# Attention and an MLP on one core: from head pairs and a polynomial GELU to token blocks and a table GELU

## The chip, the cores and the metric

The kernel runs on one core of one Trainium2 chip. The metric is the device time of one execution in microseconds, lower is better. Time before: median 383.45 us of three runs (379.78, 383.45, 383.53).

The engines of the core are named as in the profile: PE is TensorE (matmuls and transposes), DVE is VectorE, ACT is ScalarE, POOL is GpSimd, SP is SyncE, which here only issues transfers. Each engine works through its own instructions in order and waits for others through semaphores.

## What is computed

A causal linear attention with a decay per head over blocks of tokens, followed by a two-layer MLP with a tanh GELU. Four sequences of 768 tokens, 8 heads of 64 dimensions, so 3072 tokens of 512 values; the hidden layer has 2048.

```python
def _attn_ref(q, k, v, lam):
    ...
    for b in range(nb):
        intra = np.einsum('bhic,bhjc->bhij', qb, kb) * Dmask[None]
        intra = np.einsum('bhij,bhjd->bhid', intra, vb)
        inter = np.einsum('bhid,bhde->bhie', qb * lam_pow[None], kv_state)
        out[:, :, sl] = intra + inter
        kb_dec = kb * rev_pow[None]
        kv_state = lam_block[None, :, None, None] * kv_state + np.einsum('bhsd,bhse->bhde', kb_dec, vb)

def _moe_ref(x, w_in, w_out):
    h = x @ w_in
    g = 0.5 * h * (1.0 + np.tanh(c * (h + 0.044715 * h * h * h)))
    return g @ w_out
```

The reference uses blocks of 64 tokens; both kernels use blocks of 128, which gives the same result. All inputs are float32; both kernels multiply in float16 and accumulate in float32.

## The kernel before

The unit of attention is a cell: one sequence, one block of 128 tokens, one pair of heads; there are 4 x 6 x 4 = 96. For each sequence and head pair, `prep_scale` (L177) scales q and k by powers of the decay on ScalarE and casts v on GpSimd; `prep_transpose` (L190) makes 12 transposes on TensorE and copies them out of PSUM on ScalarE. `cell_stage_a` (L207) multiplies q and k of a block (two matmuls, tile Sps) and applies the causal mask on VectorE (tile PT). `cell_stage_b` (L220) makes PT times v and the carried state times q, alternating in one PSUM tile OKV for the two heads, then the new state product; VectorE updates the state and copies the result into xT, the transposed MLP input for all 3072 tokens.

The MLP runs in jobs of 512 tokens (the last two of 256). `mm1` (L262) makes four accumulating matmuls into Hps for one of 16 hidden tiles. The GELU is spread over two engines: ScalarE copies Hps to h16 (L276), VectorE squares it and forms the cubic (L278, L281), ScalarE applies a sigmoid (L290), VectorE multiplies (L292). `mm2` (L295) makes 16 accumulating matmuls for 128 tokens, ScalarE copies them out (L306), SP issues the store.

Order: `pump` (L347) takes queued MLP entries up to a budget after each cell; `jobs_after` says after which block a job is queued. A job's second layer is deferred behind the first tiles of the next job. The framework's scheduler then orders each engine's instructions by its own cost model, keeping dependences. PSUM has two buffers each for Sps and Tps together, OKV and the MLP.

Loads: SP issues q, k and v of the first sequence head pair by head pair, in pieces of 192 KB (L82), later sequences in pieces of 384 KB. The weights come through GpSimd's queue: both halves of w_in (2 MB each, L96) at the very start, w_out in four parts of 1 MB later (L102), each into a buffer that gT also uses. ScalarE casts all weights.

## Time and profile before

| | |
|---|---|
| median of three runs | 383.45 us (379.78 to 383.53) |
| span of the profiled execution, first to last instruction | 380.5 us |
| TensorE busy, instructions | 313.5 us, 1760 |
| VectorE busy, instructions | 215.1 us, 642 |
| ScalarE busy, instructions | 208.0 us, 380 |
| GpSimd busy, instructions | 21.9 us, 47 |
| moved by DMA | 33.89 MB, mean 89 GB/s |
| mean granted TensorE clock | 0.937 |

The page gives the profiled execution's span and no separate time for it. In a row of the groups, the number after the bar is busy time in us, then the mean of one instruction in ns; after the second bar stands the idle time of the engine just before these instructions and what ended it. A timeline row gives start, duration, engine, line, operation and count. A busy TensorE is not one at its peak: matmuls overlap in its pipeline, so the distance between starts gives the pace. In the table of stretches the numbers after the stretch are its length, TensorE's busy time, its instructions, the granted clock, the DMA share and GB/s.

### The profile page before, as it was taken

Reading aid. Unit: us, or ns where it says so; the run is one execution under the profiler, and the core shown is the slowest. Engines: PE = TensorE matmul, PEld = TensorE weight load, DVE = VectorE, ACT = ScalarE, POOL = GpSimd, SP = SyncE. Lnnn points to the kernel's source line nnn. Section 1 sums busy time; section 2 is a strip of 40 time slices with the busy share of each in tenths; the row PEclk is TensorE's granted clock in tenths of the full one; section 3 lists DMA queues with packets and bytes.
Section 4 is the critical chain, followed back from the end, with each engine's and each line's share of the span. In section 5 each row is a group of like instructions: output and inputs, shape, how many; then the busy total and the mean of one; then the engine's idle time right before and its main releaser. Section 6 shows DMA issues by size and latency. Waiting matters only on the chain.

```text
span 380.5 us, 5045 instructions
## 1 busy us (share of the span) xinstructions
PE 313.5 (82%) x1760; PEld 153.2 (40%) x1760; DVE 215.1 (57%) x642; ACT 208.0 (55%) x380; POOL 21.9 (6%) x47
## 2 busy tenths in 40 slices
PE   0048099897899998999997799987999987995975
PEld 0024044443344444454444244543344444453542
DVE  3005034357998089743499551489641899118683
ACT  3793666638885166778366141676331566126663
POOL 2021202312000000310000000000000000000000
PEclk9999999999999999659999579999689997899989
DMA  7999999994800990001100002000001000020101
GB/s 276 312 224 286 274 279 218 213 218 76 167 1 13 228 202 2 0 3 56 55 2 1 0 2 83 29 1 0 2 28 57 28 1 3 28 83 2 54 2 57
DMA packets 79946, 33.89 MB, mean 89 GB/s; under 512 B 75312, under 2 KB 75312, under 8 KB 79408
## 3 DMA queue, kind: packets, MB, share of 16 engines
q1 hardware_dynamic: 78288, 25.18, 31.7%
q0 software_dynamic: 1632, 8.39, 6.0%
q8 instruction: 14, 0.23, 0.3%
q14 instruction: 12, 0.10, 0.1%
HBM read 27.27 MB, written 6.29 MB: 88 GB/s over the span
## 4 chain that ended last, share of the span: by engine, by line
PE 60%; DVE 17%; ACT 8%; SPq 7%; DMA 4%; issue 2%; ACTq 0%; DVEq 0%
PE O2ps L299 18%; PE Hps L268 15%; DVE u L281 7%; SPq L82 7%; PE OKV L227 6%; PE OKV L230 6%; DVE s L278 4%; PE Tps L198 4%; PE O2ps_t L299 4%; ACT h L276 4%; PE OKV L234 3%; ACT z L290 3%; PE Sps L213 3%; DVE gT L292 2%; DMA q<-in_q_dram 2%
## 5 line engine op out<-in xcount | busy, mean ns | idle before, releaser
L268 PE MATMUL Hps<-xT,w_in 128*128 128x512 f16 (+1 forms) x332 | 94.4, 413 | 12.8 <-ACT h L276 8.8
L290 ACT ACTIVATE z<-u 128x512 f16<-128x512 f16 (+1 forms) x112 | 63.2, 568 | 46.5 <-DVE u L281 45.3
L216 DVE TENSOR_TENSOR PT<-Sps,mask_all 128x256 f16<-128x256 f32 x96 | 39.9, 417 | 62.4 <-PE Sps L213 62.2
L299 PE MATMUL O2ps<-w_out,gT 128*128 128x512 f16 x304 | 70.2, 389 | 0.0
L281 DVE SCALAR_TENSOR_TENSOR u<-s,h 128x512 f16<-128x512 f16 (+1 forms) x112 | 67.5, 613 | 1.4
L276 ACT ACTIVATE h<-Hps 128x512 f16<-128x512 f32 (+1 forms) x83 | 48.2, 585 | 26.2 <-PE Hps L268 21.8
L268 PEld LDWEIGHTS <-w_in 128*128 128x128 f16 x448 | 41.5, 101 | 49.5 <-issue 18.6
L299 PEld LDWEIGHTS <-gT 128*128 128x128 f16 x384 | 38.0, 101 | 48.5 <-issue 5.8
L278 DVE TENSOR_TENSOR s<-h 128x512 f16<-128x512 f16 (+1 forms) x112 | 43.4, 387 | 24.8 <-ACT h L276 23.2
L198 PE MATMUL Tps<-ident,a 128*128 128x128 f16 x192 | 25.0, 279 | 35.0 <-ACT a L183 29.0
L227 PE MATMUL OKV<-PT,a 128*64 128x128 f16 x192 | 47.0, 266 | 5.7 <-DVE PT L216 5.3
L292 DVE TENSOR_TENSOR gT<-z,h 128x512 f16<-128x512 f16 (+1 forms) x112 | 42.7, 382 | 14.5 <-ACT z L290 14.2
L230 PE MATMUL OKV<-qkT,kv_new 64*64 64x128 f16 x160 | 42.8, 267 | 0.3
L306 ACT ACTIVATE o<-O2ps 128x512 f32<-128x512 f32 x19 | 11.3, 596 | 50.9 <-PE O2ps L299 49.0
L243 DVE CAST xT<-OKV 128x128 f16<-128x128 f32 x96 | 27.2, 283 | 19.0 <-PE OKV L234 19.0
L200 ACT ACTIVATE qkT<-Tps 128x512 f16<-128x512 f16 x48 | 27.3, 594 | 19.1 <-PE Tps L198 18.9
L227 PEld LDWEIGHTS <-a 128*64 128x64 f16 x192 | 20.5, 115 | 34.2 <-issue 22.6
L198 PEld LDWEIGHTS <-a 128*128 128x128 f16 x192 | 16.8, 124 | 42.3 <-ACT a L183 29.4
L238 DVE SCALAR_TENSOR_TENSOR kv_new<-kv_new,lam128vec,OKV 128x64 f16<-128x64 f16 x64 | 17.7, 276 | 27.1 <-PE OKV L234 26.9
L213 PE MATMUL Sps<-qkT 64*128 64x128 f16 x192 | 24.4, 250 | 2.1 <-ACT qkT L200 2.1
L230 PEld LDWEIGHTS <-kv_new 64*64 64x64 f16 x160 | 17.8, 111 | 19.2 <-issue 5.7
L183 ACT ACTIVATE a<-q,qdscale 128x384 f16<-128x384 f32 x32 | 19.1, 606 | 9.5 <-DMA q<-in_q_dram 9.1
(37 smaller groups left out, 163.2 us busy)
## 6 DMA issues: line engine op xcount, KB each, us to landing
out_dram<-o SPq DMA_DIRECT2D x24, 256.0 KB, 2.0
q<-in_q_dram SPq DMA_DIRECT2D x12, 384.0 KB, 6.1
k<-in_k_dram SPq DMA_DIRECT2D x12, 384.0 KB, 6.3
v<-in_v_dram SPq DMA_DIRECT2D x12, 384.0 KB, 6.1
wi<-in_moe_w_in_dram POOLq DMA_DIRECT2D x2, 2048.0 KB, 11.1
wo<-in_moe_w_out_dram POOLq DMA_DIRECT2D x4, 1024.0 KB, 7.2
q<-in_q_dram SPq DMA_DIRECT2D x8, 192.0 KB, 4.5
k<-in_k_dram SPq DMA_DIRECT2D x8, 192.0 KB, 4.5
```

The source lines that it names most:

```text
L198: nc.tensor.transpose(Tps[:, bip, t, :], a16[:, t, blk, :, :], ident[:])
L213: nc.tensor.matmul(Sps[:, hl, 0:P], qkT[hpart, blk, 1, :], qkT[hpart, blk, 0, :], start=True, stop=True)
L216: nc.vector.tensor_tensor(PT[:], Sps[:, :, 0:P], mask_all[:, h0 : h0 + 2, :], ALU.mult)
L227: nc.tensor.matmul(OKV[opart, 0:P], a16[:, 2, blk, hl, :], PT[:, hl, :], start=True, stop=(blk == 0))
L230: nc.tensor.matmul(OKV[opart, 0:P], kv16[(b, hp)][opart, :], qkT[opart, blk, 0, :], start=False, stop=True)
L268: nc.tensor.matmul(Hps[:, 0:ntok], w_in16[:, c, f * P : (f + 1) * P], xT[:, c, tok0 : tok0 + ntok], start=(c == 0), stop=(c == 3))
L276: nc.scalar.activation(out=h16[:, 0:ntok], in_=Hps[:, 0:ntok], func=AF.Copy)
L278: nc.vector.tensor_tensor(s16[:, 0:ntok], h16[:, 0:ntok], h16[:, 0:ntok], ALU.mult)
L281: nc.vector.scalar_tensor_tensor(u16[:, 0:ntok], s16[:, 0:ntok], C_ADD, h16[:, 0:ntok], ALU.add, ALU.mult)
L290: nc.scalar.activation(out=z16[:, 0:ntok], in_=u16[:, 0:ntok], func=AF.Sigmoid, scale=C_SIG)
L292: nc.vector.tensor_tensor(job["gT"][:, f, 0:ntok], z16[:, 0:ntok], h16[:, 0:ntok], ALU.mult)
L299: nc.tensor.matmul(O2[:], gT[:, f, tau * P : (tau + 1) * P], w_out16[:, f, :], start=(f == 0), stop=(f == NF - 1))
```

## The change

The kernel is rewritten around steps. A step is one block of 128 tokens of one sequence over all 8 heads; there are 24. Each step has three stages: `stage_t` makes eight transposes (q and k of four head pairs) into one PSUM tile and VectorE copies it out in one instruction; `stage_s` makes eight matmuls and VectorE masks all 1024 columns in one instruction; `stage_o` makes the eight PT products, the eight state products, then the eight state-times-q products, after which VectorE updates the state (four instructions) and ScalarE copies the result to xT. Step s has stage_t of block s + 2, stage_s of s + 1 and stage_o of s. Each of these PSUM tiles has one buffer, the MLP has three.

The MLP runs per group of 512 tokens in pieces of four matmuls: 16 first-layer pieces, each with its GELU, and 16 second-layer pieces. `fill` places eight pieces in each step from the sixth on (five in the fifth), in three portions ahead of the stages. What is left runs at the end. The GELU is one ScalarE activation from PSUM to gT; h16, s16, u16 and z16 are gone. VectorE copies the second layer out, GpSimd issues the stores.

`prep` works per pair of blocks: VectorE scales q, GpSimd scales k, ScalarE casts v, one instruction per block over all heads.

```diff
-    def load_split(b, hp):
-        for hl in range(2):
-            for t_x, x in ((t_q, q), (t_k, k), (t_v, v)):
-                nc.sync.dma_start(out=t_x[:, hl], in_=x[b, h0 + hl].rearrange(
-                    "(blk p) d -> p blk d", p=P))
...
+    def load_pair(b, bp):
...
+        for j in range(2):
+            r0 = (2 * bp + j) * P
+            for t, src in zip(ts, (q, k, v)):
+                nc.sync.dma_start(out=t[:, j], in_=src[b, :, r0 : r0 + P, :].rearrange(
+                    "h p d -> p h d"))
...
+        for blk in range(2):
+            nc.vector.tensor_tensor(
+                tq[:, blk], q32[:, blk],
+                qd[:].unsqueeze(2).to_broadcast([P, H, D]), ALU.mult)
+            nc.gpsimd.tensor_tensor(
+                tk[:, blk], k32[:, blk],
+                kd[:].unsqueeze(2).to_broadcast([P, H, D]), ALU.mult)
+            nc.scalar.activation(out=tv[:, blk], in_=v32[:, blk], func=AF.Copy)
...
-            nc.tensor.matmul(OKV[opart, 0:P], a16[:, 2, blk, hl, :], PT[:, hl, :],
-                             start=True, stop=(blk == 0))
-            if blk > 0:
-                nc.tensor.matmul(OKV[opart, 0:P], kv16[(b, hp)][opart, :],
-                                 qkT[opart, blk, 0, :], start=False, stop=True)
...
+        for hp in range(NHP):
+            for hl in range(2):
+                r = slice(64 * hl, 64 * hl + 64)
+                nc.tensor.matmul(Ops[r, hp, :], tv[:, j, 2 * hp + hl, :], PT[:, hl, hp, :],
+                                 start=(hp == 0), stop=not inter, skip_group_check=True)
...
+                    nc.tensor.matmul(Ops[r, hp, :], kv[r, hp, :], o[r, 0, hp, :],
+                                     start=False, stop=True, skip_group_check=True)
...
-            nc.scalar.activation(out=h16[:, 0:ntok], in_=Hps[:, 0:ntok], func=AF.Copy)
...
-            nc.vector.tensor_tensor(s16[:, 0:ntok], h16[:, 0:ntok], h16[:, 0:ntok],
-                                    ALU.mult)
...
-            nc.vector.scalar_tensor_tensor(u16[:, 0:ntok], s16[:, 0:ntok], C_ADD,
-                                           h16[:, 0:ntok], ALU.add, ALU.mult)
...
-            nc.scalar.activation(out=z16[:, 0:ntok], in_=u16[:, 0:ntok],
-                                 func=AF.Sigmoid, scale=C_SIG)
-            nc.vector.tensor_tensor(job["gT"][:, f, 0:ntok], z16[:, 0:ntok],
-                                    h16[:, 0:ntok], ALU.mult)
...
+            nc.scalar.activation(out=gT[:, f, :], in_=Hps[:], func=AF.Gelu_apprx_tanh)
...
+                nc.vector.tensor_copy(out=o32[:], in_=O2.pop(tau)[:])
+                row0 = g * GSZ + tau * P
+                nc.gpsimd.dma_start(out=out[row0 : row0 + P, :], in_=o32[:])
...
+    stage_t(0)
+    stage_t(1)
+    stage_s(0)
+    for s in range(NSTEP):
+        backlog = len(filler)
+        n = 0 if s < 4 else (5 if s == 4 else 8)
+        if s < 4:
+            cast_win(s)
+        if 2 <= s < 6:
+            cast_wout(s - 2)
+        if s % 2 == 0 and preps:
+            prep(*preps.pop(0))
+            if loads:
+                load_pair(*loads.pop(0))
+        fill((n + 2) // 3)
+        if s + 2 < NSTEP:
+            stage_t(s + 2)
+        fill((n + 1) // 3)
+        if s + 1 < NSTEP:
+            stage_s(s + 1)
+        fill(n // 3)
+        stage_o(s)
+        if s % 4 == 3:
+            queue_group(s // 4)
+    fill(len(filler))
```

The scheduler still orders each engine's instructions, so the order is shown as it comes out, at two places.

The first is the loading at the start. Before, GpSimd's queue had both halves of w_in (wi) ahead of everything, beside SP's loads of q, k and v:

```order
L96 DMA wi_0_135<-in_moe_w_in_dram 128x2x2048
L96 DMA wi_1_137<-in_moe_w_in_dram 128x2x2048
masks.py:197 MEMSET ident 128x128
L116 ISA
L116 IOTA posp_146 128x1
masks.py:199 AFFINE_SELECT ident<-ident 128x128
L119 IOTA pos_148 128x1
L145 IOTA rel 128x128
L187 CAST a_0_0_185<-v_0_0_101 128x6x64 x2
L187 CAST a_0_1_213<-v_0_1_110 128x6x64 x2
L102 DMA wo_0_366<-in_moe_w_out_dram 128x4x512
```

Now all loads are SP's. The names give sequence and pair of blocks (q_0_2 is the third pair of sequence 0); the first two pairs and three quarters of w_in stand ahead of this piece. In brackets stands what a load waits for; the DMAHW entries are earlier transfers whose semaphore it takes over (eight are in flight), Activation and Pool are the casts that free a weight buffer:

```order
L76 DMA wi_3_182<-in_moe_w_in_dram 128x4x512 [waits DMAHW5_49,DMAHW0_49,Activation_49]
L66 DMA q_0_2_184<-in_q_dram 128x8x64 [waits DMAHW1_49]
L66 DMA k_0_2_185<-in_k_dram 128x8x64 [waits DMAHW2_49]
L66 DMA v_0_2_186<-in_v_dram 128x8x64 [waits DMAHW3_49]
L66 DMA q_0_2_184<-in_q_dram 128x8x64 [waits DMAHW4_49]
L66 DMA k_0_2_185<-in_k_dram 128x8x64
L66 DMA v_0_2_186<-in_v_dram 128x8x64 [waits DMAHW6_49]
L82 DMA wo_0_193<-in_moe_w_out_dram 128x4x512 [waits DMAHW7_49,Activation_49]
L82 DMA wo_1_195<-in_moe_w_out_dram 128x4x512 [waits DMAHW0_49,Activation_49]
L82 DMA wo_2_197<-in_moe_w_out_dram 128x4x512 [waits DMAHW1_49,Activation_49]
L82 DMA wo_3_199<-in_moe_w_out_dram 128x4x512 [waits DMAHW7_49,DMAHW2_49,Pool_49]
L66 DMA q_1_0_201<-in_q_dram 128x8x64 [waits DMAHW3_49]
```

The weights moved from the front of one queue to the middle of the other, behind q, k and v of the blocks that are needed first, and four of their loads now wait for a cast.

The second place is ScalarE in the middle of the program. Before, two instructions per hidden tile (h, then z, which waits for VectorE's u) and the copies of the second layer (o):

```order
L290 ACTIVATE z_1130<-u_1110 128x512
L276 ACTIVATE h_1174<-Hps 128x512
L276 ACTIVATE h_1200<-Hps 128x512
L290 ACTIVATE z_1206<-u_1178 128x512
L290 ACTIVATE z_1367<-u_1204 128x512
L276 ACTIVATE h_1361<-Hps 128x512
L306 ACTIVATE o_1241<-O2ps 128x512
L290 ACTIVATE z_1403<-u_1365 128x512
```

Now, one GELU per hidden tile in runs (gT from Hps), with the copies to xT and the casts of v between them:

```order
L240 ACTIVATE gT_1308<-Hps 128x512 x8
L150 ACTIVATE v_3_0_1520<-v_3_0_904 128x512
L226 ACTIVATE xT_1414<-Ops 128x4x128
L150 ACTIVATE v_3_0_1520<-v_3_0_904 128x512
L240 ACTIVATE gT_1308<-Hps 128x512 x3
L226 ACTIVATE xT_1414<-Ops 128x4x128
L150 ACTIVATE v_3_1_1721<-v_3_1_1124 128x512
```

ScalarE's row no longer returns to a tile after VectorE has worked on it, and the second layer's copies have left it for VectorE.

More of the change, by code (lines that the diff above doesn't have):

```diff
@@ L106 @@
[L106 to L107 removed]
+    load_pair(0, 0)
+    load_pair(0, 1)
     ident = const.tile([P, P], FP16)
     make_identity(nc, ident)
[L112 to L113 removed]
     posp1 = const.tile([P, 1], FP32)
@@ new lines, with stage_s @@
+    PTs = {}
+    def stage_s(s):
+        o = qkT[s]
+        Sps = ps_S.tile([P, 2, NHP, P], FP32, tag="S", name="Sps")
+        for hp in range(NHP):
+            for hl in range(2):
+                r = slice(64 * hl, 64 * hl + 64)
+                nc.tensor.matmul(Sps[:, hl, hp, :], o[r, 1, hp, :], o[r, 0, hp, :],
+                                 start=True, stop=True)
+        PT = ptp.tile([P, 2, NHP, P], FP16, tag="PT", name=f"PT_{s}")
+        nc.vector.tensor_tensor(PT[:], Sps[:], mask[:], ALU.mult)
+        PTs[s] = PT
```

443 lines of the change are left out of this document (151 added, 292 removed).

## The prediction

> **What bounds the kernel now.** I read the page first (engine shares, the slices, the chain of work that ended last), then the groups of instructions with shapes kept apart, then TensorE's timeline at places where nothing waits, then the start.
>
> ```profile
> span 380.5 us, 5045 instructions
> PE 313.5 (82%) x1760; PEld 153.2 (40%) x1760; DVE 215.1 (57%) x642; ACT 208.0 (55%) x380; POOL 21.9 (6%) x47
> PEclk9999999999999999659999579999689997899989
> PE 60%; DVE 17%; ACT 8%; SPq 7%; DMA 4%; issue 2%; ACTq 0%; DVEq 0%
> ```
>
> TensorE carries 60% of the chain. The other 40% is what it waits for: VectorE and ScalarE (25%, the GELU) and loads (11%, the start). Five dips of the clock show in the slices, each late in a GELU phase.
>
> ```profile
> L268 PE MATMUL Hps<-xT,w_in 128*128 128x512 f16 x320 | 92.2, 417 | 11.1 <-ACT h L276 7.0 <-DVE xT L243 3.6
> L281 DVE SCALAR_TENSOR_TENSOR u<-s,h 128x512 f16<-128x512 f16 x80 | 53.9, 689 | 0.4
> L290 ACT ACTIVATE z<-u 128x512 f16<-128x512 f16 x80 | 49.9, 629 | 35.2 <-DVE u L281 34.8
> L276 ACT ACTIVATE h<-Hps 128x512 f16<-128x512 f32 x80 | 47.0, 592 | 25.9 <-PE Hps L268 21.8 <-DVE gT L292 2.9 <-DVE PT L216 0.3
> L278 DVE TENSOR_TENSOR s<-h 128x512 f16<-128x512 f16 x80 | 34.2, 427 | 18.8 <-ACT h L276 17.3
> L292 DVE TENSOR_TENSOR gT<-z,h 128x512 f16<-128x512 f16 x80 | 33.5, 419 | 8.8 <-ACT z L290 8.5
> L216 DVE TENSOR_TENSOR PT<-Sps,mask_all 128x256 f16<-128x256 f32 x96 | 39.9, 417 | 62.4 <-PE Sps L213 62.2
> L243 DVE CAST xT<-OKV 128x128 f16<-128x128 f32 x96 | 27.2, 283 | 19.0 <-PE OKV L234 19.0
> ```
>
> One hidden tile needs 0.59 + 0.63 = 1.22 us of ScalarE and 0.43 + 0.69 + 0.42 = 1.54 us of VectorE, hopping between the two. VectorE's 1.54 us is longer than the four matmuls that feed it, so these phases run at VectorE's pace.
>
> **What TensorE itself needs.** The starts of rows that follow each other give the pace; durations hold a latency that overlaps.
>
> ```profile
> 285.30 0.24 PE L227 MATMUL OKV<-PT,a 128*64 128x128 f16 x1
> 285.47 0.24 PE L230 MATMUL OKV<-qkT,kv_new 64*64 64x128 f16 x1
> 286.14 3.63 PE L299 MATMUL O2ps<-w_out,gT 128*128 128x512 f16 x16
> 289.70 0.23 PE L213 MATMUL Sps<-qkT 64*128 64x128 f16 x2
> 289.86 0.24 PE L227 MATMUL OKV<-PT,a 128*64 128x128 f16 x1
> ...
> 177.12 0.25 PE L227 MATMUL OKV<-PT,a 128*64 128x128 f16 x2
> 177.19 0.20 PE L234 MATMUL OKV<-a 128*64 128x64 f16 x2
> 177.32 3.63 PE L299 MATMUL O2ps<-w_out,gT 128*128 128x512 f16 x16
> ...
> 247.64 0.62 PE L198 MATMUL Tps<-ident,a 128*128 128x128 f16 x8
> 248.10 0.59 PE L268 MATMUL Hps<-xT,w_in 128*128 128x512 f16 x2
> ...
> 90.67 1.04 PE L268 MATMUL Hps<-xT,w_in 128*128 128x512 f16 x4
> 91.64 0.23 PE L213 MATMUL Sps<-qkT 64*128 64x128 f16 x1
> ```
>
> Second-layer matmuls: (289.70 - 286.14)/16 = 0.2225 us. First-layer ones in fours: (91.64 - 90.67)/4 = 0.2425. Eight transposes 0.46, a pair of S 0.16, a pair of state products (L234) 0.13. A pair of PT products (L227) in a row 0.07; alternated with the kv product (L230), 0.17 for each.
>
> **The change, part by part.**
>
> MLP matmuls. 384 + 384 of 512 columns: 384 x 0.2425 + 384 x 0.2225 = 178.5 us. The amount of work is as before.
>
> GELU. h, s, u, z and gT become one activation out of PSUM. L276 (PSUM source, 592 ns) and L290 (a table function, 629 ns) bound it; I take 0.63. Against four matmuls of 0.97 us ScalarE has room: per step of 128 tokens it has four GELUs, one xT copy and one v cast, some 6 x 0.6 = 3.7 us. VectorE loses 1.54 us per tile and gains the q scaling (f32, by the slope of L216 and L243, 1.05 ns an element, 512 elements: 0.69), the copy out of Tps and the mask product (1024 elements: 1.22 each), four state updates and the output copy (by the same slope 0.9 and 0.7): under 5 us a step. The step has 7.4 us of MLP matmuls plus attention, so neither engine is the bound. What still can stop TensorE is a Hps buffer not yet free: that wait stood at 7.0 us (L268 row, <-ACT). With three buffers in place of two, 0 is the low end; with a GELU queued behind an xT copy and a v cast, more than before can be. I keep 7.
>
> Attention, per step: eight transposes, eight S, eight PT products, eight state products, eight kv products. 0.46 + 4 x 0.16 + 4 x 0.13 = 1.62 us for three of them. PT and kv products now stand eight alike in a row instead of alternating. Bounds: 0.07 a pair (0.28 each eight) and 0.17 a matmul (1.36 each eight). I take 0.07 a matmul (0.56 each eight), nearer the pair, as the neighbours are alike. Step: 2.74 us, between 2.2 and 4.3. Steps 4 to 23: 54.8, less 4 for the state and kv products that the first and last block of a sequence lack: 51 us. Each S, PT and Ops waits on work a whole step (10 us) older, so I cost these waits at nothing; the cover is the eight pieces of MLP, and steps 0 to 3 have none.
>
> The start. Steps 0 to 3 have no MLP beside them, and weights come behind q, k, v.
>
> ```profile
> lam_bc<-in_lam_dram SPq DMA_DIRECT2D x1, 4.0 KB, 2.7
> 2.83 9.07 SPq L82 DMA_DIRECT2D q<-in_q_dram  x1
> 15.99 0.84 SPq L82 DMA_DIRECT2D q<-in_q_dram  x1
> ...
> 27.72 1.10 SPq L82 DMA_DIRECT2D k<-in_k_dram  x1
> ...
> 9.91 3.71 ACT L161 ACTIVATE w_in<-wi 128x2048 f16<-128x2048 f32 x2 [4.62 <-DMA wi<-in_moe_w_in_dram]
> 15.75 1.91 ACT L161 ACTIVATE w_in<-wi 128x2048 f16<-128x2048 f32 x1 [2.13 <-DMA wi<-in_moe_w_in_dram]
> 16.99 0.50 POOL L187 CAST a<-v 128x384 f16<-128x384 f32 x1 [13.26 <-DMA v<-in_v_dram]
> 34.61 1.03 PE L268 MATMUL Hps<-xT,w_in 128*128 128x512 f16 x2
> ```
>
> Before, SP's fourth load stuck for 9.07 us behind GpSimd's weight loads, and nothing of attention began until 17 us; the first MLP matmul ran at 34.6. From 15.99 to 27.72 SP issued 13 loads of 192 KB: 0.90 us each, so 1.2 us per load of 256 KB and 7.2 us for the six of a pair of blocks. Both weight loads (4.2 MB) were in by 15.75: 3.6 us per MB. Now two pairs land by 1.2 + 14.4 + 2.7 = 18.3 us. Behind the last block of them: the k scaling on GpSimd (the cast row gives 0.67 us for 512 elements with one input; with two I take up to 1.35), transposes 0.5, copy 1.22, S 0.64, mask 1.22, PT and kv 1.1, xT 0.6, hand-overs: 25.3. The cast of the first weight quarter stands behind that xT copy on ScalarE: 1.9 more. First MLP matmul at 27 us (24 to 34.6, the old place).
>
> The Trainium skill's GPSIMD Engine Reference (4.1, Engine selection) speaks against putting this scaling on GpSimd: two-input elementwise work there is about twice as slow as on VectorE, 4497 ns for 2048 elements. By that an estimate is 1.1 us for 512, inside the bounds above, and the sum would move by under half a microsecond.
>
> What is queued behind the new waits: SP's load of weight quarter 3 waits for ScalarE's cast of quarter 0, and behind it on SP stand all further loads. Quarter 3 lands at 33.5, blocks 4 and 5 at 41, w_out at 45, 48, 52, 55, the next sequence's first pair at 62; GpSimd then has output issues ahead of k scaling, so step 7 ends near 71. TensorE by then has 128 MLP matmuls (29.8) and four steps (11) to do from 27 on: 68 without clock loss. The two meet within 5 us, so I cost the late loads at nothing more; later, a pair per 20 us of TensorE is 7.2 us of transfer.
>
> The clock.
>
> ```profile
> 150.00:155.00 5.00, 3.97 (x28) 1.00 0.00 0
> 155.00:160.00 5.00, 4.43 (x25) 0.57 0.00 0
> 165.00:170.00 5.00, 5.00 (x30) 0.56 0.00 2
> 170.00:175.00 5.00, 5.00 (x28) 1.00 0.02 7
> ...
> 83.55 3.62 PE L268 MATMUL Hps<-xT,w_in 128*128 128x512 f16 x8
> 86.96 0.86 PE L198 MATMUL Tps<-ident,a 128*128 128x128 f16 x8
> ```
>
> After a stretch with TensorE busy 3.97 of 5 us the granted clock (third number) fell to half and stayed there some 14 us although TensorE was busy throughout. In the start the column reads 1.00, but eight matmuls took 3.41 us, 0.43 each: half rate too. So the new first group starts at half rate; with TensorE then kept busy I charge 10 us at half, a loss of 5, and no later dips (low 0; high 24, five dips of 10 us as now).
>
> The Trainium skill (TensorE: Matmul & The Clock Gate, What's actually happening) says one busy window of about 3.4 us restores the clock. The 14 us above do not agree; by the page the loss would be 1.7 us and the sum 3 us less.
>
> The end.
>
> ```profile
> 367.71 8.59 PE L299 MATMUL O2ps_t<-w_out,gT 128*128 128x512 f16 x32
> ```
>
> Last matmul at 376.3, span 380.5: 4.2 us for the last copy and store, kept at 4.5 since the store is now issued by GpSimd.
>
> **Sum.** 27 + 178.5 + 51 + 7 + 5 + 4.5 = 273 us of span. The profiled span is 380.5, the median time 383.45 (runs 379.78 to 383.53); the same 3 us on top give 276 us.
>
> **Rivals.**
>
> Late loads and casts starve the start: the chain SP, ScalarE's casts, GpSimd's casts opens four holes of a load's 2.7 to 3.6 us instead of one, step 7 ends at 84 rather than 71, and the pause costs one more dip of the clock: 276 + 11 + 5 = 292. For it: SP is strictly in order and one weight buffer too few. Against it: TensorE has work until 68.
>
> PT and kv products stay at 0.17 each: 40 x (1.36 - 0.56) = 32 less a little, 306. For it: every alternated row shows 0.17. Against it: the pair at 0.07.
>
> The change doesn't do what it says: the scheduler gathers the pieces in runs, and attention's stages stand next to each other without cover. Then a copy or a mask product of 1.22 us, less what overlaps, lies open in each of 20 steps: 20 us, 296. For it: the scheduler moves instructions freely, and the first group's pieces do stand in a run. Against it: from the second group on the new order has two or three pieces between stages, eight in each step.
>
> Slower: the clock stays at half. For it: long half-rate stretches without any pause. Then 768 x 0.427 = 328, attention 51 x 1.4 = 71, and 27 + 7 + 4.5: 438 of span. A half-rate matmul costs 0.2 us more, so slower than before needs some 535 of the 768 at half rate. Against it: every dip ended under dense work (170, and four like it).
>
> **Chances.** Forecast 0.70; starved start 0.13; 0.17 products 0.06; gathered pieces 0.07; half clock 0.04. The range reaches from 256 (attention at 2.2 a step, no waits) to 305 (starved start and one or two more dips). About 1% is what a measurement can tell from no change; all but the last rival are faster by far, so faster 0.95, same 0.01, slower 0.04.
>
> **What would show it.** First MLP matmul near 27 us; span per step 10 us once loads are ahead; ScalarE's GELU at 0.6 us; no TensorE wait above 2 us after 75 us; clock 1.00 after 45 us. It is wrong if PT products start 0.17 apart, if steps take 12 us or more (then VectorE or GpSimd is late), or if the first group's second layer waits for w_out.

## The result, and the profile after

The changed kernel takes 243.5 us (median of 4 runs, 243.09 to 243.75) against 381.62 us of the kernel before in the same job: a ratio of 0.6385 (95% interval 0.635 to 0.6419). The forecast was 276 us, with a range from 256 to 305. The direction was right, but the time lies below the range: the gain is 138 us where about 107 were expected. The clock in the records is 1.000 over the whole span of 242.0 us, with no dips; the matmuls of the start ran at half rate all the same, as their pace shows further down.

The page after: instructions and busy time, the clock by slices, the chain of work that ended last, and the groups that answer to those shown of before.

```profile
span 242.0 us, 3956 instructions
PE 216.9 (90%) x1664; PEld 107.0 (44%) x1664; DVE 99.6 (41%) x174; ACT 94.6 (39%) x156; POOL 48.4 (20%) x61
PEclk9999999999999999999999999999999999999999
PE 45%; issue 37%; ACT 5%; DVE 4%; POOL 3%; DMA 2%; SPq 1%; POOLq 0%; DVEq 0%
L238 PE MATMUL Hps<-xT,w_in 128*128 128x512 f16 x384 | 91.7, 387 | 4.0 <-ACT w_in L87 2.5
L240 ACT ACTIVATE gT<-Hps 128x512 f16<-128x512 f32 x96 | 56.8, 598 | 39.9 <-PE Hps L238 39.7
L179 DVE TENSOR_TENSOR PT<-Sps,mask 128x1024 f16<-128x1024 f32 x24 | 29.4, 1224 | 31.5 <-PE Sps L176 31.5
L147 POOL TENSOR_TENSOR k<-k,kd 128x512 f16<-128x512 f32 x24 | 26.3, 1105 | 56.8 <-DMA k<-in_k_dram 30.5
L165 DVE COPY qkT<-Tps 128x1024 f16<-128x1024 f16 x24 | 16.5, 687 | 26.7 <-PE Tps L162 26.7
```

TensorE was 82% busy and is 90% busy, with VectorE down from 215.1 to 99.6 us and ScalarE from 208.0 to 94.6. In the chain TensorE holds 45%. The 37% of "issue" is not its own: from 143 us on, the chain goes along GpSimd's stores (POOL L254), and these pieces lie between one store and the next, with no wait shown. TensorE is busy there nearly all the time, as the row for 90 to 237 us shows (length, busy time and count of TensorE, then the other engines, clock, DMA share, GB/s):

```profile
90.00:237.00 147.00, 146.84 (x1068) 70.28 (x1065) 55.12 (x94) 52.43 (x91) 21.32 (x29) 1.00 0.32 79
```

ScalarE's GELU waits for TensorE in nearly all its idle time (39.7 of 39.9 us), as it should if TensorE is the bound. But TensorE's own need has also fallen, from 313.5 us busy to 216.9 (part of the 313.5 was at half clock), though it does the same MLP. That is the part that the forecast got wrong.

One step of 128 tokens, in TensorE's timeline. Columns: start, busy time of the group, line, what it writes and reads, shapes, count.

```profile
129.22 0.41 PE L196 MATMUL Ops<-PT,v 128*64 128x128 f16 x8
129.46 0.29 PE L203 MATMUL Kps<-v,k 128*64 128x64 f16 x8
129.69 0.41 PE L211 MATMUL Ops<-qkT,kv 64*64 64x128 f16 x8
130.03 2.76 PE L248 MATMUL O2ps<-w_out,gT 128*128 128x512 f16 x12
132.63 0.39 PE L162 MATMUL Tps<-ident,q 128*128 128x128 f16 x4
132.85 0.39 PE L162 MATMUL Tps<-ident,k 128*128 128x128 f16 x4
133.07 2.75 PE L248 MATMUL O2ps<-w_out,gT 128*128 128x512 f16 x12
135.76 0.40 PE L176 MATMUL Sps<-qkT 64*128 64x128 f16 x8
136.09 1.90 PE L248 MATMUL O2ps<-w_out,gT 128*128 128x512 f16 x8
137.92 0.25 PE L196 MATMUL Ops<-PT,v 128*64 128x128 f16 x2
```

A step takes 137.92 - 129.22 = 8.70 us; some 10.2 were forecast. From start to start, the five kinds of attention products take 0.24, 0.23, 0.34, 0.44 (both rows of transposes) and 0.33: 1.58 us, where the forecast had 2.74. The numbers behind the output's name (128\*64, 64\*64, 128\*128, 64\*128) are the rows and columns of the array that a matmul uses, its tile shape. Compare the three stretches of MLP. Twelve matmuls before the transposes, which have the MLP's own shape 128\*128, take 132.63 - 130.03 = 2.60, so 0.217 each. Twelve before the scores, 64\*128, take 2.69; eight before the values products, 128\*64, take 1.83, where eight times 0.217 is 1.74. Each change of shape leaves about 0.1 us; the step from Ops to Kps (both 128\*64) and the one from MLP to transposes leave none.

### The profile page after: what moved, and what is told of

The parts are those of the page before. It is cut to its first block, busy times and chain, and to the rows that moved or that the text cites. A ratio compares the mean times of both kernels' runs of the same rounds, so it can differ in the third digit from the quotient of the medians.

```text
span 242.0 us, 3956 instructions
## 1 busy us (share of the span) xinstructions
PE 216.9 (90%) x1664; PEld 107.0 (44%) x1664; DVE 99.6 (41%) x174; ACT 94.6 (39%) x156; POOL 48.4 (20%) x61
## 4 chain that ended last, share of the span: by engine, by line
PE 45%; issue 37%; ACT 5%; DVE 4%; POOL 3%; DMA 2%; SPq 1%; POOLq 0%; DVEq 0%
PE Hps L238 17%; PE O2ps L248 16%; PE Tps L162 4%; ACT w_in L87 3%; PE Ops L196 3%; POOL out_dram L254 2%; PE Sps L176 2%; PE Ops L211 2%; DVE PT L179 2%; DMA v<-in_v_dram 2%; ACT gT L240 1%; POOL k L147 1%; DVE q L144 1%; DVE qkT L165 1%; ACT xT L226 1%
## 5 line engine op out<-in xcount | busy, mean ns | idle before, releaser
L238 PE MATMUL Hps<-xT,w_in 128*128 128x512 f16 x384 | 91.7, 387 | 4.0 <-ACT w_in L87 2.5
L248 PE MATMUL O2ps<-w_out,gT 128*128 128x512 f16 x384 | 88.1, 380 | 0.0
L240 ACT ACTIVATE gT<-Hps 128x512 f16<-128x512 f32 x96 | 56.8, 598 | 39.9 <-PE Hps L238 39.7
L248 PEld LDWEIGHTS <-gT 128*128 128x128 f16 x384 | 35.7, 98 | 40.6
L179 DVE TENSOR_TENSOR PT<-Sps,mask 128x1024 f16<-128x1024 f32 x24 | 29.4, 1224 | 31.5 <-PE Sps L176 31.5
L226 ACT ACTIVATE xT<-Ops 128x512 f16<-128x512 f32 x24 | 14.3, 595 | 69.3 <-PE Ops L211 52.0
L254 POOL DMA_DIRECT2D out_dram<-o x24 | 13.5, 561 | 125.9 <-DVE o L252 125.8
L147 POOL TENSOR_TENSOR k<-k,kd 128x512 f16<-128x512 f32 x24 | 26.3, 1105 | 56.8 <-DMA k<-in_k_dram 30.5
L252 DVE COPY o<-O2ps 128x512 f32<-128x512 f32 x24 | 16.5, 687 | 48.9 <-PE O2ps L248 48.9
L144 DVE TENSOR_TENSOR q<-q,qd 128x512 f16<-128x512 f32 x24 | 23.9, 1000 | 16.9 <-DMA q<-in_q_dram 16.3
L165 DVE COPY qkT<-Tps 128x1024 f16<-128x1024 f16 x24 | 16.5, 687 | 26.7 <-PE Tps L162 26.7
L150 ACT ACTIVATE v<-v 128x512 f16<-128x512 f32 x24 | 14.8, 624 | 17.6 <-DMA v<-in_v_dram 9.7
L196 PEld LDWEIGHTS <-v 128*64 128x64 f16 x192 | 7.1, 117 | 11.7 <-issue 10.2
L162 PE MATMUL Tps<-ident,q 128*128 128x128 f16 x96 | 10.2, 234 | 2.1 <-DVE q L144 1.3
L162 PE MATMUL Tps<-ident,k 128*128 128x128 f16 x96 | 10.2, 235 | 0.0
```

Of the source, the lines that this page charges most:

```text
L144: nc.vector.tensor_tensor(tq[:, blk], q32[:, blk], qd[:].unsqueeze(2).to_broadcast([P, H, D]), ALU.mult)
L147: nc.gpsimd.tensor_tensor(tk[:, blk], k32[:, blk], kd[:].unsqueeze(2).to_broadcast([P, H, D]), ALU.mult)
L162: nc.tensor.transpose(Tps[:, i, hp, :], t[:, j, 2 * hp : 2 * hp + 2, :], ident[:])
L165: nc.vector.tensor_copy(out=o[:], in_=Tps[:])
L179: nc.vector.tensor_tensor(PT[:], Sps[:], mask[:], ALU.mult)
L196: nc.tensor.matmul(Ops[r, hp, :], tv[:, j, 2 * hp + hl, :], PT[:, hl, hp, :], start=(hp == 0), stop=not inter, skip_group_check=True)
```

## The experiments

Fourteen kernels were run. All times are medians; ratios are against the kernel before in the same job. "Changes of shape" are counted in the order of TensorE's instructions: 596 in the kernel before, 125 in the changed one.

| run | us | changes of shape |
|---|---|---|
| before | 381 to 384 | 596 |
| e5 before + single GELU | 341.49 | 589 |
| e6 before + runs | 358.3 | 369 |
| e9 before + both | 300.88 | 359 |
| after | 243.5 | 125 |
| e1 after, O and I alternated | 294.6 | 411 |
| e2 after, K and I alternated | 269.94 | 279 |
| e3 after, O and K alternated | 243.77 | 125 |
| e13 after, MLP pieces between heads | 265.14 | 319 |

### Does the order of the attention products cost time? (e1, e2, e3)

O is the product of values with PT (128\*64), K the state product (128\*64), I the product of the old state with q (64\*64). Theory A puts the price on a change of tile shape; its rivals put it on the place in PSUM, on any alternation, or elsewhere. Alternating O with I changes shape and shares a place in PSUM; K with I changes shape and shares none; O with K keeps the shape.

```diff
         for hp in range(NHP):
...
                 nc.tensor.matmul(Ops[r, hp, :], tv[:, j, 2 * hp + hl, :], PT[:, hl, hp, :],
...
+                if inter:
+                    nc.tensor.matmul(Ops[r, hp, :], kv[r, hp, :], o[r, 0, hp, :],
+                                     start=False, stop=True, skip_group_check=True)
...
-        if inter:
-            kv = kvd[b]
-            for hp in range(NHP):
...
```

(e2 puts the same lines behind each K product; e3 puts each K product behind its O product.)

> The changed kernel with one edit: in each step the PT product and the state-times-q product of a head stand next to each other, as before the change, instead of eight of one kind and then eight of the other. In the new order TensorE changes the kind of its matmuls 471 times instead of 196. Theory A (a change of the tile shape in the array, 128x64 to 64x64, costs about 0.13 us, since alternated rows stood 0.17 us apart and rows in a run of one kind stand 0.03 to 0.04 apart): 20 steps x 16 x 0.13 = 43 us, less what lies in the starved first 70 us: span 270 to 285. Theory B (the second product waits for the first because both add into the same place in PSUM): the same 270 to 285. Theory C (any alternation of two kinds costs it): the same. Rival D (the 0.17 us before the change came from something else there): 242 to 246. This run tells A, B and C from D.

> The changed kernel with the state products (128x64) and the state-times-q products (64x64) alternated; they write different places in PSUM. 350 changes of kind instead of 196, 16 steps. A (change of shape): 16 x 16 x 0.13 = 33 us, less the starved part: span 262 to 275. B (same place in PSUM): 242 to 246. C (any alternation): 262 to 275.

> The changed kernel with the PT products and the state products alternated: both have 128 rows and 64 columns of weights, different places in PSUM. 377 changes of line instead of 196, but no change of shape beyond those of the changed kernel. A: 242 to 246. B: 242 to 246. C: 20 x 16 x 0.13 = 42, span 270 to 285.

Measured: e1 294.6 us (ratio 0.7672, 0.7566 to 0.7778), above the 270 to 285 of A, B and C; e2 269.94 (0.7062, 0.7004 to 0.712), where A and C had it and B did not; e3 243.77 (0.6375, 0.6323 to 0.6426), where A and B had it and C did not. TensorE's timeline of e1, then of e3:

```profile
159.70 0.24 PE L197 MATMUL Ops<-PT,v 128*64 128x128 f16 x1
159.88 0.24 PE L200 MATMUL Ops<-qkT,kv 64*64 64x128 f16 x1
160.04 0.24 PE L197 MATMUL Ops<-PT,v 128*64 128x128 f16 x1
...
162.45 0.32 PE L207 MATMUL Kps<-v,k 128*64 128x64 f16 x8
```

```profile
120.53 0.25 PE L198 MATMUL Ops<-PT,v 128*64 128x128 f16 x2
120.61 0.20 PE L201 MATMUL Kps<-v,k 128*64 128x64 f16 x2
...
121.00 0.41 PE L209 MATMUL Ops<-qkT,kv 64*64 64x128 f16 x8
```

In e1 sixteen products take 162.45 - 159.70 = 2.75 us, 0.17 each; in runs of a kind the same sixteen take 0.24 + 0.34 = 0.58. In e3 O and K alternate, their starts in twos; sixteen products take 121.00 - 120.53 = 0.47 us, as in runs (0.24 + 0.23), and nothing is lost. So a shared place in PSUM is not needed for the loss (e2), and alternation alone is free (e3).

A product in e1 costs 0.13 us more than in a run (0.17 less 0.04). Not all of it need be the change of shape. In a run, the trace's single records have the two products of a head pair 0.004 us apart and the next pair 0.052 behind: the two run side by side. In e1 and e2 a product of the other shape stands between them, and each starts alone. If one alone takes 0.055 us, as a transpose does, also of 128 columns (eight in 0.44), 0.115 is left for the change. e1 and e2 can't tell the two apart; e13 below keeps the pairs whole, has 194 more changes, and finds 0.111 each. With it, A stands. The Trainium skill has the rule (TensorEngine Tiling (Array Packing), Tiling Modes, Key Properties): a change of tiling mode, not merely of the tile, drains TensorE. It gives no price; e3's and e13's rows agree with the rule and supply one.

e1 lost 51 us for 286 more changes, 0.18 each, more than the 0.13 of the rows, which gives 37 us. Most of the rest is the clock: e1's mean of 0.971 over 293.5 us is 8.5 us lost. Two windows of e1 show a dip (busy time and count of each engine, then the granted clock, DMA share, GB/s):

```profile
145.00:150.00 5.00, 5.00 (x41) 2.69 (x40) 1.23 (x1) 1.81 (x4) 0.00 (x0) 1.00 0.00 0
150.00:155.00 5.00, 5.00 (x29) 2.24 (x28) 1.69 (x5) 3.20 (x6) 2.49 (x2) 0.66 0.01 3
```

A row of alternated products ended at 149.88, and the clock dropped right behind it, though TensorE's records show it busy for the whole of both windows. e2's mean clock is 0.979, e3's 0.999.

### What is the single GELU worth? (e4, e5)

e4 is the changed kernel with the GELU of before (h, s, u, z and a product, on ScalarE and VectorE):

```diff
-            nc.scalar.activation(out=gT[:, f, :], in_=Hps[:], func=AF.Gelu_apprx_tanh)
+            nc.scalar.activation(out=h16[:], in_=Hps[:], func=AF.Copy)
+            nc.vector.tensor_tensor(s16[:], h16[:], h16[:], ALU.mult)
+            nc.vector.scalar_tensor_tensor(u16[:], s16[:], C_ADD, h16[:], ALU.add, ALU.mult)
+            nc.scalar.activation(out=z16[:], in_=u16[:], func=AF.Sigmoid, scale=C_SIG)
+            nc.vector.tensor_tensor(gT[:, f, :], z16[:], h16[:], ALU.mult)
```

> The changed kernel with the GELU of before (copy, square, cubic, sigmoid, product; four buffers for each in-between tile). VectorE then has 1.54 us more per hidden tile. Theory 1 (the GELU sets the pace where first-layer pieces stand, as in the kernel before): in the two steps out of four that hold first-layer pieces VectorE has 24.6 + 7.2 = 32 us against TensorE's 17.4, six times 14 us: span 305 to 330, with stretches at half the granted clock. Rival 2 (interleaving spreads it, only VectorE's sum counts: 39 us per group against 35): span 262 to 275, clock 1.00.

Measured: 280.57 us (ratio 0.7347, 0.7289 to 0.7405), between the two theories: 37 us more than the changed kernel. VectorE comes to 231.2 us, and the longest of TensorE's waits (in us, times, the longest) shows where it holds:

```profile
PE Hps L241 <- ACT h L244: 18.7, 15, 4.8
```

e5 is the reverse edit, the single GELU in the kernel before.

```diff
-            nc.scalar.activation(out=h16[:, 0:ntok], in_=Hps[:, 0:ntok], func=AF.Copy)
...
+            nc.scalar.activation(out=job["gT"][:, f, 0:ntok], in_=Hps[:, 0:ntok],
+                                 func=AF.Gelu_apprx_tanh)
```

> The kernel before with one edit: the GELU is the single table activation out of PSUM. If the GELU's five instructions set the pace of its first-layer phases: most of the 42 us in which TensorE stood idle goes, and part of the 24 us of half clock; span 310 to 335. If the small attention matmuls and the start are the larger part: above 350.

Measured: 341.49 us (ratio 0.8956, 0.8894 to 0.9019), again between the theories. From both sides the single GELU is worth 37 to 40 us, the dips of the clock that go with it included (0.977 in e4, 1.000 in the changed kernel). With it the kernel before waits for no other engine but in the start: TensorE's waits there are 31.2 us in three waits for scaled q, and the next entry is 2.8. So the other 98 us between e5 and the changed kernel are not the GELU.

### The products in runs, alone and together with the GELU (e6, e9)

e6 writes the products of a head pair in the kernel before as O, O, K, K, I, I:

```diff
             nc.tensor.matmul(OKV[opart, 0:P], a16[:, 2, blk, hl, :], PT[:, hl, :],
-                             start=True, stop=(blk == 0))
-            if blk > 0:
-                nc.tensor.matmul(OKV[opart, 0:P], kv16[(b, hp)][opart, :],
-                                 qkT[opart, blk, 0, :], start=False, stop=True)
+                             start=True, stop=(blk == 0), skip_group_check=True)
...
+        if blk > 0:
+            for hl in range(2):
+                opart = slice(64 * hl, 64 * hl + 64)
+                nc.tensor.matmul(OKV[opart, 0:P], kv16[(b, hp)][opart, :],
+                                 qkT[opart, blk, 0, :], start=False, stop=True,
+                                 skip_group_check=True)
```

> The kernel before with one edit: in each cell the two PT products, the two state products and the two state-times-q products stand in this order, instead of PT, state-times-q, PT, state-times-q, state, state. Three changes of tile shape fewer in each of 80 cells. Theory (a change of shape costs about 0.13 us, and long stretches of such changes bring the clock down): 31 us, less where TensorE waits for VectorE anyway: span 350 to 368. Rival (TensorE isn't the bound where cells stand): 378 to 383.

Measured: 358.3 us (ratio 0.9392, 0.9332 to 0.9452), as A expected. But there TensorE also waits for the other engines, so the size of A's price is not clean in it. e9 joins this edit with e5's, where it waits for nothing after the start:

> The kernel before with the single GELU and with the products O, O, K, K, I, I of a head pair in runs: the edits of two earlier runs (341.5 and 358.3 us alone) together. With the single GELU alone TensorE waits for nothing after the start. Theory A (each change of tile shape between neighbouring matmuls costs 0.13 to 0.17 us): the order has 359 changes of shape instead of 589, so 230 x 0.13 to 0.17 = 30 to 39 us less, 302 to 312 us. Rival (the runs of one kind gained 23 us alone because TensorE then waited less for the other engines): nothing is left to gain here, 335 to 342 us.

Measured: 300.88 us (ratio 0.7865, 0.7826 to 0.7903), just below A's 302 to 312 and far from the rival. The runs are worth 40.6 us with the GELU single and 23 alone: alone, part of their gain went into waiting: TensorE's waits sum to 79 us in e6 and to 62 in the kernel before. One head pair of one block in TensorE's timeline, first of e5, then of e9:

```profile
250.54 0.24 PE L227 MATMUL OKV<-PT,a 128*64 128x128 f16 x1
250.72 0.24 PE L230 MATMUL OKV<-qkT,kv_new 64*64 64x128 f16 x1
250.89 0.24 PE L227 MATMUL OKV<-PT,a 128*64 128x128 f16 x1
251.06 0.24 PE L230 MATMUL OKV<-qkT,kv_new 64*64 64x128 f16 x1
251.23 0.22 PE L234 MATMUL OKV<-a 128*64 128x64 f16 x2
251.38 0.23 PE L213 MATMUL Sps<-qkT 64*128 64x128 f16 x2
251.54 0.60 PE L268 MATMUL Hps<-xT,w_in 128*128 128x512 f16 x2
```

```profile
250.24 0.23 PE L213 MATMUL Sps<-qkT 64*128 64x128 f16 x2
250.40 0.25 PE L227 MATMUL OKV<-PT,a 128*64 128x128 f16 x2
250.48 0.20 PE L231 MATMUL OKV<-a 128*64 128x64 f16 x2
250.60 0.24 PE L237 MATMUL OKV<-qkT,kv_new 64*64 64x128 f16 x2
250.78 1.68 PE L272 MATMUL Hps<-xT,w_in 128*128 128x256 f16 x12
```

The same eight products take 251.54 - 250.54 = 1.00 us in e5 and 250.78 - 250.24 = 0.54 us in e9. Between the MLP matmuls on either side there are seven changes of shape in e5 and four in e9: 0.46 us for three, 0.15 each. e5 also breaks the two O and the two I apart, so part of this is again the pairs. Over the whole kernel, 40.6 us for 230 fewer changes is 0.177 each, but that holds a dip of the clock that e9 doesn't have (0.978 in e5, 0.998 in e9): from 195 to 215 us e5's clock reads 0.67, 0.50, 0.50 and 0.97 in stretches of 5 us, about 7 us lost. Without it, it is 0.146 each.

### Are changes between MLP and attention dear too? (e13)

57 us were still open between e9 and the changed kernel. e13 keeps the changed kernel's instructions, tiles and edges and only places the eight MLP pieces of a step one behind each head pair's scores and values products, rather than in three portions:

```diff
+    def drip():
+        if quota[0] and filler:
+            quota[0] -= 1
+            filler.pop(0)()
...
                 nc.tensor.matmul(Sps[:, hl, hp, :], o[r, 1, hp, :], o[r, 0, hp, :],
                                  start=True, stop=True)
+            drip()
...
-        fill((n + 2) // 3)
+        quota[0] = n
```

> The changed kernel with the eight MLP pieces of a step not in three portions but one behind each head pair's scores and each head pair's values products, near to how the kernel before mixed them. All instructions, tiles and waits of the other engines stay. Changes of tile shape rise from 125 to 319. Theory A (a change costs 0.11 to 0.15 us beside an MLP matmul too): 194 x 0.11 to 0.15 = 21 to 29 us more, 264 to 273 us, and most of what separates the kernel before with both edits (300.9 us) from the changed one is this. Rival (only a change between two small products costs; an MLP matmul of 0.22 us covers it): 244 to 250 us, and those 57 us lie elsewhere.

Measured: 265.14 us (ratio 0.6919, 0.6882 to 0.6956), 21.6 more than the changed kernel for 194 more changes: 0.111 each, inside A's range. The waits of the other engines are as in the changed kernel, and the two products of a pair stay together. TensorE's timeline of e13:

```profile
150.65 0.23 PE L183 MATMUL Sps<-qkT 64*128 64x128 f16 x2
150.81 1.04 PE L256 MATMUL O2ps<-w_out,gT 128*128 128x512 f16 x4
151.78 0.23 PE L183 MATMUL Sps<-qkT 64*128 64x128 f16 x2
```

Four MLP matmuls take 0.97 us, the very number that the forecast read in the kernel before; four times 0.217 is 0.87, and the 0.10 that is left is the change. A mean of 0.2425 each is not the matmul's price but that of its company.

### What do the order of loads and the portions bring? (e7, e8, e10)

e7 runs each group's MLP in one piece after its fourth attention step (output weights cast two steps earlier); e8 issues the weight loads first on GpSimd's queue, as the kernel before did, with four staging buffers; e10 puts all eight pieces of a step ahead of its attention.

```diff
# e7
-        n = 0 if s < 4 else (5 if s == 4 else 8)
+        n = 0
...
             queue_group(s // 4)
+            fill(len(filler))
# e8
-        nc.sync.dma_start(out=t[:], in_=moe_w_in[:, j * 512 : (j + 1) * 512].rearrange(
+        nc.gpsimd.dma_start(out=t[:], in_=moe_w_in[:, j * 512 : (j + 1) * 512].rearrange(
...
+    for j in range(4):
+        load_win(j)
     load_pair(0, 0)
# e10
-        fill((n + 2) // 3)
+        fill(n)
...
-        fill((n + 1) // 3)
...
-        fill(n // 3)
```

> The changed kernel with no MLP pieces placed in the steps: after each fourth step the whole group follows in a run; the output weights are cast two steps earlier. The work is the same. If the pieces are the cover of attention's copies and masks: a bare step took 3.3 to 4.4 us in the first four steps, 1.6 us of it TensorE's, so 20 steps x 2 to 2.8 us: span 280 to 300, with half clock at the beginning of groups. If buffers and the scheduler's freedom give the cover anyway: 242 to 255.

> The changed kernel with all weights on GpSimd's queue again, w_in ahead of everything, four staging buffers. The bytes are the same. If the order of loads at the start carries little: the first step's q, k and v come some 8 us later, but the hole in the transfers at 25 to 30 us goes: span 242 to 252. If the start of the kernel before came from this order: first MLP matmul near 35 or later instead of 29, and attention of the first steps after it: 252 to 262.

> The changed kernel with all eight MLP pieces of a step ahead of its attention instead of in three portions. Changes of tile shape fall from 125 to 111, 14 x 0.13 = 1.8 us: theory A without a new wait gives 241 to 243 us. Rival (the portions cover VectorE's copy and mask product, 0.69 + 1.22 us per step, which then stand open in some steps): 248 us or more.

Measured: e7 259.18 us (ratio 0.6794, 0.6733 to 0.6856), between its two theories: 15.7 us lost. The copies and mask products that the pieces covered now stand open; of TensorE's waits in e7 the row that grew most:

```profile
PE Sps L176 <- DVE PT L179: 7.2, 13, 1.3
```

It stood at 1.0 us, once, in the changed kernel. TensorE's waits together are some 8 us longer, about half of the loss. The clock shows the other part: it dips to half in e7 (mean 0.972, which is 7 us of 257.3), and not in the changed kernel.

e8: 262.03 us (ratio 0.687, 0.6828 to 0.6912), 18.5 lost; its span of 259.8 lies inside the second theory's 252 to 262. SP's timeline, then TensorE's, of e8:

```profile
3.65 11.59 SPq L66 DMA_DIRECT2D q<-in_q_dram  x1
```

```profile
30.34 0.61 PE L164 MATMUL Tps<-ident,q 128*128 128x128 f16 x4 [30.34 <-DVE q L146]
```

SP is stuck at its fourth load of q, k and v again, as in the kernel before (9.07 us there, 11.59 here), and the first transposes start at 30.34 instead of 10.09. How far had the kernels come by 90 us? One window of the changed kernel, then of e9 (length, TensorE's busy time and count, clock, DMA share, GB/s), and how e9 goes on from there:

```profile
0.00:90.00 90.00, 70.06 (x600) 1.00 1.04 244
```

```profile
0.00:90.00 90.00, 49.25 (x361) 1.00 1.10 251
90.00:298.00 208.00, 204.28 (x1401) 99.27 (x1398) 54.62 (x200) 91.66 (x174) 4.81 (x10) 1.00 0.21 54
```

The data moved at about the same rate; in the changed kernel it came in the order of use. Busy time is no measure of the work here, as e9 ran at half rate for most of the window though the clock column reads 1.00. Its MLP matmuls show it, before 79 us and behind:

```profile
76.28 3.29 PE L272 MATMUL Hps<-xT,w_in 128*128 128x512 f16 x8
79.41 0.28 PE L198 MATMUL Tps<-ident,a 128*128 128x128 f16 x2
...
80.49 1.89 PE L272 MATMUL Hps<-xT,w_in 128*128 128x512 f16 x8
82.31 0.28 PE L213 MATMUL Sps<-qkT 64*128 64x128 f16 x4
```

Eight take 3.13 us first and 1.82 then. Counted in the traces, the changed kernel had started 192 of its 768 MLP matmuls by 90 us, e9 only 55. From there on both run at full clock and wait for nearly nothing, so what is left to do gives the 57 us, as an estimate. e9 has the work of 137 more MLP matmuls before it (counting two of 256 columns as one), 30 us at 0.217, and 134 more attention products and transposes, 5 us at 0.04. It also has 197 more changes of shape before it (263 against 66), 22 us at e13's 0.111. So some 35 of the 57 us were lost in the first 90 us and some 22 go to the changes. e8 had started 128 MLP matmuls by 90 us: the order of the loads, put back into the changed kernel, brings about half of the 35. The other half wasn't tried apart.

e10: 242.3 us (ratio 0.6341, 0.6319 to 0.6363), 1.2 us less than the changed kernel for 14 fewer changes, as A expected; the intervals of the two ratios touch, so by itself this run shows only that no new wait came.

### A better version (e11, e12, e14)

In the start SP is held at the fourth weight load until the first cast frees a buffer, and the DMA engines stand nearly idle from 25 to 30 us (share 0.09). With three buffers, five of the eight weight loads wait for a cast, as the order at the start shows. e11 has five staging buffers. e12 adds a first weight cast in four parts, and stores from ScalarE's queue. e14 takes e12's two additions and e10's single portion, with three buffers.

```diff
# e11, e12
-    wst = ctx.enter_context(tc.tile_pool(name="wst", bufs=3))
+    wst = ctx.enter_context(tc.tile_pool(name="wst", bufs=5))
# e12, e14
+        for i in range(4 if j == 0 else 1):
+            w = 128 if j == 0 else 512
+            nc.scalar.activation(out=w_in16[:, :, j * 512 + i * w : j * 512 + (i + 1) * w],
+                                 in_=t[:, :, i * w : (i + 1) * w], func=AF.Copy)
...
-                nc.gpsimd.dma_start(out=out[row0 : row0 + P, :], in_=o32[:])
+                nc.scalar.dma_start(out=out[row0 : row0 + P, :], in_=o32[:])
# e14
-        fill((n + 2) // 3)
+        fill(n)
```

> The changed kernel with five staging buffers for weights instead of three, so that SP's queue is not held at the fourth weight load. If the late loads behind that wait make the stretch from 60 to 72 us in which TensorE is not full: 237 to 241 us. If that stretch comes from the work of GpSimd and VectorE (scaling of q and k behind stores on GpSimd's queue): 242.5 to 244.5 us, no change.

> The changed kernel with five staging buffers, the first input weight cast in four parts of a quarter (so that the first MLP matmul waits for a quarter of 1.9 us) and the output stores issued from ScalarE's queue instead of GpSimd's. Start 1.4 us earlier by the cast; if the stores on GpSimd's queue held the scaling of k in the stretch from 60 to 72 us, 2 us more: 237 to 241 us. If neither is on the path, or the stores hold ScalarE's queue in turn: 242 to 246 us.

> The parts that gained, without the part that lost: first input weight cast in four parts, stores on ScalarE's queue, all eight pieces of a step in one portion, three staging buffers as in the changed kernel. If the gains of the one portion (1.2 us) and of the other two (3.0 us with five buffers, which alone cost 2.6 us) add up: 236 to 239 us. If the five buffers were needed for the earlier start or the stores: 240 to 243 us.

Measured: e11 246.09 us (ratio 0.6437, 0.641 to 0.6464), above both expected ranges; its median is 2.6 us above the changed kernel's, though the intervals touch. The hole in the transfers is gone (share 1.13 from 25 to 30 us), but TensorE then waits for VectorE's scaling of q (3.0 us in two waits; 1.3 in one in the changed kernel). Letting the late loads start sooner gained nothing. e12 is 240.43 us (0.6297, 0.6273 to 0.632) and e14 238.84 us (0.6231, 0.6204 to 0.6259): faster than the changed kernel by 1% and 2%, and the five buffers were not needed. What the stores' queue did shows in GpSimd's and VectorE's rows, first in the changed kernel, then in e12:

```profile
62.71 0.54 POOL L254 DMA_DIRECT2D out_dram<-o  x1 [0.63 <-DVE o L252]
63.27 2.05 POOL L147 TENSOR_TENSOR k<-k,kd 128x512 f16<-128x512 f32 x2
63.52 2.35 DVE L144 TENSOR_TENSOR q<-q,qd 128x512 f16<-128x512 f32 x1
```

```profile
59.18 1.04 POOL L150 TENSOR_TENSOR k<-k,kd 128x512 f16<-128x512 f32 x1 [2.19 <-PE O2ps L251]
62.97 0.68 DVE L147 TENSOR_TENSOR q<-q,qd 128x512 f16<-128x512 f32 x1
```

VectorE's scaling of q takes 0.68 us alone and 2.35 us when it meets two scalings of k on GpSimd: it ends just after they do. The k scaling stood behind stores on GpSimd's queue, which wait for VectorE's copy; with the stores on another queue it ran earlier and the two didn't meet. The Trainium skill (SBUF — State Buffer, Who interferes with whom) says that a VectorE instruction with two SBUF inputs contends with a GpSimd one that reads SBUF, and calls the ports that the two share an exclusive lock; the rows agree.

## Why the prediction fell short

- **Attention per step: 2.74 us forecast, 1.58 measured.** This is the step that failed. The forecast took 4 x 0.16 for eight scores and 4 x 0.13 for eight state products, from pairs in the kernel before. Both prices held a change of shape, paid once per pair there and once per run of eight here: 0.33 and 0.23 measured. e9 and e13 show that price. For values products and state-times-q products it chose 0.07 each, which is twice the pace of the pair it quoted (two in 0.07): 0.56 per eight, 0.24 and 0.34 measured. So of the 1.16 us that are too much, 0.60 is the change charged four times over and 0.54 this choice. Over 20 steps it is some 21 us. The low end, 2.2 us, was built from the same pairs and so was no bound. The quoted rows held the answer: two values products in 0.07 with a product of the same shape behind them, two state products in 0.13 with an MLP matmul behind them.
- **MLP: 0.2425 and 0.2225 us forecast.** The same fault: 0.2425 is 0.217 and a quarter of a change. In the new step 32 matmuls take 2.60 + 2.69 + 1.83 = 7.12 us, 0.2225 with its changes, so the first layer was charged 384 x 0.02 = 8 us too much. The second layer's price was right.
- **The rival of 0.17 a product** did not come: that pace needs alternated shapes, and the new order has runs. e1 made it so and came to 294.6 us, where the forecast gave 306.
- **GELU:** 0.63 forecast, 0.598 measured; off the bound as said, worth 37 to 40 us (e4, e5). The wait for a free Hps, kept at 7 us, fell to about 1 us on ScalarE's GELU.
- **The start:** 27 us forecast, 29.28 measured, by the chain that was named, with the first cast behind the fourth xT copy (ScalarE, 27.33 to 29.23). But the loads came sooner and the steps took longer than forecast: the last k was being scaled at 16.92 already, where 18.3 was forecast for its landing. The four xT copies then stand at 16.74, 19.40, 22.38 and 26.83, steps that queue behind each other, where the forecast followed the last block alone. SP was held at the fourth weight load as named. Scaling k on GpSimd took 1.105 us, inside the bounds of 0.67 to 1.35. The estimate of 1.1 that was worked out from the Trainium skill (GPSIMD Engine Reference, 4.1, Engine selection; the 4497 ns that it rests on stand in 3.1, Elementwise) agrees. That it would slow VectorE's scaling of q beside it was not foreseen; in the stretch from 60 to 72 us, where the two meet, TensorE is busy 9.82 us in the changed kernel and 11.10 in e14, where they don't.
- **The clock:** a loss of 5 us charged, 2.2 measured: the first sixteen MLP matmuls take 5.83 us, where sixteen at full rate took 3.63 before (the clock column reads 1.00 for both). That there would be no dip after the start was right. The estimate of 1.7 us worked out from the Trainium skill (TensorE: Matmul & The Clock Gate, What's actually happening) was nearer than the 5.
- **Cover:** that the MLP pieces hide the waits of attention was right; without them 15.7 us come back (e7). The rival of a starved start did not come; e11, where the late loads come sooner, is not faster.
- **The end:** 4.5 forecast, 5.1 measured.

With these sizes in its own sum the forecast comes to 273 - 21 - 8 - 3 (clock) + 2 (start) + 1 (end) = 244 us of span, and some 3 us less for the waits that did not come, against 242.0 measured.

## What to carry to other kernels

Order small matmuls on TensorE by tile shape before anything else: each change of rows and columns between neighbours cost 0.10 to 0.15 us here, as much as three or four small products in a run, and alternating kinds of one shape cost nothing. Keep the two heads of a pair next to each other as well: their products ran side by side. When a price per instruction is read from a timeline, take it from runs of two lengths, so that what is paid per run and what is paid per instruction come apart. Measure progress in matmuls done and not in busy time, which half rate stretches. And when a change removes the stall of one engine, look at whether the waiting hid another cost: the products in runs were worth 23 us beside the old GELU and 41 without it.

## What the runs showed of the hardware

- The cost of a change of tile shape: 0.10 to 0.11 us beside MLP matmuls with the pairs whole (e13), about 0.115 as an estimate between small products (e1, 0.13 with what the broken pairs cost), none between different tensors of one shape (e3).
- The two products of a head pair, which write different halves of the partitions, start 0.004 us apart in a run, the next pair 0.052 behind (changed kernel, values products from 129.22).
- The first matmuls of these kernels ran at half rate, though the clock column reads 1.00 there: in the changed kernel this ended within the first sixteen MLP matmuls, in e9, whose MLP matmuls come late, only at about 79 us.
- The clock fell to half behind stretches of alternated small products, with TensorE's records busy throughout (e1: 0.66 in the window from 150 us, mean 0.971). The kernel e9, which differs from e5 in those stretches alone, has 0.998 against 0.978. What brings the clock down can't be told from these runs.
- A copy from PSUM of 1024 16-bit elements took VectorE 0.687 us, though a mask product of 1024 elements from 32-bit PSUM took 1.224; the forecast had 1.22 for both.
- VectorE's two-input scaling took 0.68 us alone and 2.35 us beside GpSimd's.
